# Value projection of 14 of 16 blocks by seven products in place of eight, woven with the gate matmuls

## The chip, the cores and the metric

One core of one Trainium2 chip. The metric is the device time of a whole launch in microseconds. Executions of one kernel mostly lie within 0.3% of each other on one chip, and the times compared below are of the same rounds on the same chip; where runs of different rounds are set beside each other, it is by their ratios to the kernel before. The span of a profile runs from the first to the last instruction and is some 2 us shorter than the time of the launch.

## The reference, cut to what matters

```python
# attention with projected keys and values: batch 8, 8 heads, 1024 positions, head 64
k_proj = np.einsum('ks,bhsd->bhkd', E, k);  v_proj = np.einsum('ks,bhsd->bhkd', F, v)
scores = 1/np.sqrt(64) * np.matmul(q, k_proj.transpose(0, 1, 3, 2))
attn = softmax(scores);  x = np.matmul(attn, v_proj)          # then 8192 tokens x 512
# gated feed-forward
gate = 1.0 / (1.0 + np.exp(-(x @ w_gate)))                     # 512 x 1536
val = x @ w_val                                                # 512 x 1536
out = gate * val @ w_out                                       # 1536 x 512
```

## The kernel before

The 8192 tokens are 16 blocks of 512, two blocks to a batch. Every operation is put on one list with the data that it reads and writes; each engine then runs its own part of that list in order and waits on semaphores where the data demand it. While TensorE works on the feed-forward of batch b, the attention of batch b + 1 is laid between its steps. PSUM, the memory that TensorE writes its products to, is used as eight banks: four for the feed-forward (`ffn`, shown as pF), four for the attention (`att`, shown as pA).

The step for one tile of 128 features makes gate and value with eight matmuls of 512 columns:

```python
def mstep(blk, m):
    pbs = {n: ffn.next() for n in "GV"}
    for n in "GV":
        for i in range(NI):                       # NI = 4
            mm_one(blk, m, i, n, pbs[n])          # W[:, i, m] x xT[:, i, half, 512 tokens]
    gate(blk, m, pbs["G"], pbs["V"])              # ScalarE: sig = tanh(0.5 g); VectorE: hT = (sig + 1) * v
```

The output projection of 14 blocks already goes by seven products: `first_products` and `last_products` make sums and differences of quarters of hT and w_out, run seven products of 12 matmuls of 256 columns in two banks, a and c, and copy a bank out between products of the same chain (`keep_snap` on ScalarE, `add_snap` on VectorE, into `ost`, which then is stored).

Keys and values of a batch are projected, copied and turned so:

```python
def kv(b, bk): ...                      # TensorE: 16 matmuls read the K and V buffers
def keep_kd(bk):
    act(kpd, bank[bk][0:64], ...)       # ScalarE: a copy of the projected keys
    add("SP", dma_start_transpose(kpD, kpd), dma="kpD")    # a small transposing transfer
# loads of the next K, V, Q: issued by GpSimd as soon as the buffers have been read
def load_k(b):
    load(KV[0], k[b]..., r=turned() if b >= 2 else ())     # also after the transposes of Q have landed
# [cut]
put(3, kv2)                             # batch 1: K/V product of batch 2, ahead of the output products
put(4 if b == 1 else 1, lambda: load_next(b + 2))
```

The softmax here doesn't subtract the row's maximum and nothing guards it: scores larger than these inputs give would overflow.

## Time and profile before

| | before |
|---|---|
| time, median of 3 (range) | 547.77 us (547.4 to 548.25) |
| span, granted clock | 545.4 us, 1.00 |
| TensorE, VectorE, ScalarE, GpSimd busy | 97%, 56%, 43%, 21% |
| one period (one batch) in the steady part | 64.6 us |

The page's busy line, the chain and TensorE's timeline stand in the prediction below. In a timeline a row is start, length, engine, line, operation, output <- inputs, shapes and count; in square brackets is how long the engine sat idle ahead of it and what released it. A hint for reading: matmul lengths overlap, so the pace is the difference of the starts.

### The profile page before, as it was taken

To read this page: it belongs to the slowest core of one execution; us is meant where nothing else is said; L and a number is where in the kernel's file an instruction comes from. 1 tells how busy PE (TensorE), PEld (TensorE's weight loads), DVE (VectorE), ACT (ScalarE), POOL (GpSimd) and SP (SyncE) were. 2 spreads that over 40 slices of the span, in tenths; PEclk is the share of its full clock that TensorE was granted. 3 is DMA by queue.
4 is the path that set the end of the run, shared out by engine and by line. 5 is a ranking of instruction groups with operands and counts; after the bars stand their busy time and mean duration, and the time that the engine had idled before them with its cause. 6 is when DMAs were issued, how large, how long until landed. Compare 5 with 4: busy or idle time off the path is not lost.

```text
span 545.4 us, 8923 instructions
## 1 busy us (share of the span) xinstructions
PE 530.7 (97%) x3504; PEld 298.7 (55%) x3561; DVE 305.5 (56%) x499; ACT 232.1 (43%) x414; POOL 113.5 (21%) x148
## 2 busy tenths in 40 slices
PE   5999999999999999999999999999999999999998
PEld 4544445646565474644647465564656547474654
DVE  4645386346863559437583466734785375834432
ACT  2654823465335633365333753346533562323330
POOL 9310200103800055000830019000350007100000
PEclk9999999999999999999999999999999999999999
DMA  9999998983795117960286502953020202001022
GB/s 159 200 195 201 163 209 176 153 178 49 148 201 127 31 21 150 152 156 11 79 137 131 121 12 78 185 144 59 13 78 1 78 0 81 2 7 72 1 77 78
DMA packets 76570, 56.09 MB, mean 103 GB/s; under 512 B 34704, under 2 KB 68240, under 8 KB 76528
## 3 DMA queue, kind: packets, MB, share of 16 engines
q0 software_dynamic: 33984, 29.89, 35.4%
q1 hardware_dynamic: 42544, 25.63, 18.6%
q8 instruction: 28, 0.46, 0.4%
q14 instruction: 14, 0.11, 0.1%
HBM read 60.29 MB, written 16.78 MB: 141 GB/s over the span
## 4 chain that ended last, share of the span: by engine, by line
PE 93%; DMA 2%; DVE 1%; ACT 1%; issue 1%; POOL 1%; POOLq 0%
PE pF L227 88%; PE pA L227 5%; DMA KV<-in_v_dram 2%; DVE hT L1063 0%; DVE rden L822 0%; POOL KV L245 0%; POOL Qb L245 0%; ACT xu L231 0%; ACT vpD L231 0%; ACT sig L231 0%; ACT eT L231 0%; ACT kpd L231 0%; DVE rden L602 0%; DVE hS L1138 0%; DVE xT L651 0%
## 5 line engine op out<-in xcount | busy, mean ns | idle before, releaser
L1063 DVE SCALAR_TENSOR_TENSOR hT<-sig,pF 128x512 bf16<-128x512 f32 x192 | 130.6, 681 | 118.9 <-PE pF L227 75.1
L227 PE MATMUL pF<-xT,wV 128*128 128x512 bf16 x752 | 195.6, 379 | 1.2 <-DVE hT L1063 0.3
L227 PE MATMUL pF<-xT,wG 128*128 128x512 bf16 x729 | 191.2, 379 | 3.1 <-issue 1.3
L231 ACT ACTIVATE sig<-pF 128x512 f32<-128x512 f32 x192 | 116.1, 605 | 171.2 <-PE pF L227 146.6
L896 POOL PARTITION_BROADCAST rb<-eT x96 | 77.1, 864 | 279.6 <-DMA eT<-rden 274.5
L227 PEld LDWEIGHTS pF<-xT,wV 128*128 128x128 bf16 x768 | 75.0, 98 | 90.9 <-DVE hT L1063 1.0
L227 PEld LDWEIGHTS pF<-xT,wG 128*128 128x128 bf16 x768 | 72.6, 98 | 88.6 <-issue 9.0
L227 PE MATMUL pF<-wO,hT 128*128 128x256 bf16 (+3 forms) x610 | 80.8, 287 | 0.1
L227 PEld LDWEIGHTS pF<-wO,hT 128*128 128x128 bf16 x612 | 59.2, 98 | 19.7 <-issue 0.8
L1183 DVE SCALAR_TENSOR_TENSOR ost<-pF,EF 128x512 f32<-128x512 f32 x28 | 19.4, 692 | 51.4 <-PE pF L227 48.8
L227 PE MATMUL pF<-wT,hT 128*128 128x256 bf16 x336 | 41.2, 273 | 0.0
L927 DVE TENSOR_TENSOR xT<-xu,rb 128x512 bf16<-128x512 f32 x48 | 40.3, 878 | 0.0
L227 PE MATMUL pF<-wT,hS 128*128 128x256 bf16 x336 | 39.0, 273 | 0.3 <-ACT EF L231 0.3
L231 ACT ACTIVATE EF<-pF 128x512 f32<-128x512 f32 x28 | 16.7, 597 | 47.0 <-PE pF L227 46.9
L227 PEld LDWEIGHTS pF<-wT,hT 128*128 128x128 bf16 x336 | 32.9, 98 | 6.8
L227 PEld LDWEIGHTS pF<-wT,hS 128*128 128x128 bf16 x336 | 32.8, 98 | 4.3 <-ACT EF L231 0.6
L822 DVE RECIPROCAL rden<-pA 128x128 f32<-128x128 f32 x26 | 24.6, 950 | 9.5 <-PE pA L227 9.5
L1183 DVE SCALAR_TENSOR_TENSOR ost<-pF,snap 128x512 f32<-128x512 f32 x14 | 9.7, 692 | 35.6 <-PE pF L227 25.0
L231 ACT ACTIVATE xu<-pA 128x512 f32<-128x512 f32 x46 | 25.2, 617 | 1.1 <-PE pA L227 1.1
L231 ACT ACTIVATE snap<-pF 128x512 f32<-128x512 f32 x14 | 8.4, 597 | 28.3 <-PE pF L227 28.3
L231 ACT ACTIVATE eT<-pA 128x512 bf16<-128x512 f32 x35 | 19.3, 622 | 1.0 <-PE pA L227 1.0
L231 ACT ACTIVATE eT<-pF 128x512 bf16<-128x512 f32 x29 | 15.8, 594 | 8.3 <-PE pF L227 8.2
(93 smaller groups left out, 268.5 us busy)
## 6 DMA issues: line engine op xcount, KB each, us to landing
out_dram<-ost SPq DMA_DIRECT2D x63, 256.0 KB, 2.4
Qb<-in_q_dram POOLq DMA_DIRECT2D x7, 1024.0 KB, 17.8
KV<-in_k_dram POOLq DMA_DIRECT2D x7, 1024.0 KB, 9.8
KV<-in_v_dram POOLq DMA_DIRECT2D x7, 1024.0 KB, 14.0
wO<-in_moe_w_out_dram POOLq DMA_DIRECT2D x1, 1536.0 KB, 11.9
wG<-in_moe_w_gate_dram POOLq DMA_DIRECT2D x5, 256.0 KB, 18.2
wV<-in_moe_w_val_dram POOLq DMA_DIRECT2D x5, 256.0 KB, 18.8
KV<-in_k_dram POOLq DMA_DIRECT2D x2, 512.0 KB, 8.8
```

The costliest lines, as they stand in the source:

```text
L227: return add("PE", lambda e: e.matmul(o, lhsT, rhs, **kw), r=r, x=[("bank", b)])
L231: return add("ACT", lambda e: e.activation(o, i, func, scale=scale), r=r, w=w, x=x)
L822: lambda e: e.reciprocal(rden[:, cc], bank[bk][:, cc]),
L896: lambda e, n=n, i=2 * rnd + c, j=j, parts=parts: e.partition_broadcast(rb[0:parts, n, :], rrow[32 * j : 32 * j + 1, i, :], channels=parts),
L927: lambda e: e.tensor_tensor(xT[s][:, r, :, 256 * g : 256 * g + 256], xu[:, n, :].rearrange("p (f c) -> p f c", f=2), y.rearrange("p (f c) ...
L1063: lambda e: e.scalar_tensor_tensor(hT[blk % 2][:, m, :], sg[:, :], 1.0, bank[pv][:, :], ALU.add, ALU.mult,),
L1183: lambda e: e.scalar_tensor_tensor(o, bank[bk][:, :].rearrange("p (j c) -> p j c", j=2), 0.5, snap[n].rearrange("p (j c) -> p j c", j=2), ...
```

## The change

The intent: values of a unit (four feature tiles of a block) by seven products of 4 matmuls of 256 columns in place of 16 matmuls of 512, from batch 1 on: 14 blocks x 3 units. With A the quarters of x and B the quarters of w_val, S1 = A21 + A22, S2 = S1 - A11, S3 = A11 - A21, S4 = A12 - S2, T1 = B12 - B11, T2 = B22 - T1, T3 = B22 - B12, T4 = B21 - T2. The products go into two banks a and c, between gate steps:

```diff
+        def v_pieces(K):          # condensed: several statements to a line
+            def p1():
+                v_product(blk, q, a, "A11", "B11", start=True);  v_snap(0, a)
+            def p26():
+                v_product(blk, q, c, "A12", "B21", start=True, stop=True);  v_add(0, c)
+                v_product(blk, q, a, "S2", "T2");  v_snap(1, a)
+                hidden(K, 0, 0, vsnap[0][:, :], [("vsnap", 0)])
+            def p57():
+                v_product(blk, q, c, "S1", "T1", start=True)
+                v_product(blk, q, a, "S3", "T3");  v_snap(2, a);  v_add(2, c)
+            def p4():
+                v_product(blk, q, a, "A22", "T4", stop=True)
+                hidden(K, 0, 1, bank[a][:, :], [], b=a);  hidden(K, 1, 1, vsnap[2][:, :], ...)
+            def p3():
+                v_product(blk, q, c, "S4", "B22", stop=True);  v_add(1, c)
+                hidden(K, 1, 0, vsnap[1][:, :], [("vsnap", 1)])
+                todo += [last_piece, p1, g_step(K, 1), p26, g_step(K, 2), p57,
+                         g_step(K, 3), p4, g_step(K + 1, 0)]; last_piece = p3
```

`v_snap` is a ScalarE copy of the bank, `v_add` a VectorE addition of bank and copy, `hidden` the gate multiply, now mostly with two SBUF operands. Sums of x (`xs_sums`), of w_val (`vt_sums`, once) and of hT (`s_sums`) all run on VectorE, most of them laid where TensorE runs the output products. To make room, the broadcast rows `rb` share the K/V buffer, early constants share one buffer, and the denominators go in eight groups. The schedule is written anew, and with it the start of batch 1 (condensed too):

```diff
-                put(3, kv2)
-                put(4 if b == 1 else 1, lambda b=b: load_next(b + 2))
+                on(0, 0, lambda: first_products(o0, first))
+                on(0, 2, lambda: last_products(o0))
+                    on(0, 2, kv2)
+                    on(0, 3, lambda: keep_kd(held_v["kv"]))
+                load_at = (1, 4) if b == 1 else (0, 2)
+                on(*load_at, lambda: (load_k(b + 2), load_v(b + 2), load_q(b + 2)))
+                on(4, 4, lambda: (mul(0, 0), mul(0, 1)))      # attention multiplies, unit 4
+                last = {-1: mul(1, 0), 0: (mul(1, 1), mul(2, 0), mul(2, 1)), 1: (mul(3, 0), mul(3, 1))}
```

(The first number of `on` is the unit within the batch, the second the slot within the unit. Of the full diff the buffers, the first batch and the helper functions are cut.)

## The prediction

> **What bounds the kernel now.** I read the page's busy line and chain first, then TensorE's timeline in one steady period, then what the other engines do there.
>
> ```profile
> PE 530.7 (97%) x3504; PEld 298.7 (55%) x3561; DVE 305.5 (56%) x499; ACT 232.1 (43%) x414; POOL 113.5 (21%) x148
> ...
> PE 93%; DMA 2%; DVE 1%; ACT 1%; issue 1%; POOL 1%; POOLq 0%
> ```
>
> The first line alone would not settle it, since a busy TensorE may still be badly fed. The second does: 93% of the chain that ended last is matmuls following matmuls, and 2% a load at the start. The chain repeats every 64.6 us (a mstep stretch starts at 187.92 and again at 252.51), one period for each batch, which is two blocks of values, gates and output plus the attention of the next batch. The timeline of TensorE (start, length, instruction) shows the pace inside:
>
> ```profile
> 257.48 2.78 PE L227 MATMUL pF<-wO,hT 128*128 128x256 bf16 x24
> 260.10 2.78 PE L227 MATMUL pF<-wT,hS 128*128 128x256 bf16 x24
> ...
> 274.42 1.03 PE L227 MATMUL pF<-xT,wV 128*128 128x512 bf16 x4
> 275.28 1.03 PE L227 MATMUL pF<-xT,wG 128*128 128x512 bf16 x4
> ```
>
> Read the starts, not the lengths. 24 matmuls of 256 columns take 260.10 - 257.48 = 2.62 us, 109.2 ns each. Four of 512 columns take 0.865 us (two such groups take 1.73), 216.2 ns each. There is no gap between groups. A period adds up: 192 x 0.2162 (gates and values) + 168 x 0.1092 (output products) = 41.5 + 18.3 = 59.9 us, and the remaining 4.7 us are the attention's own matmuls. So stalls are nearly nil and only fewer columns, without new gaps, can make it faster.
>
> **What the Trainium skill says.** "TensorE: Matmul & The Clock Gate", section Back-to-back issue gap, gives 518 cycles for 512 columns and 262 for 256 at 2.4 GHz, 216 and 109 ns: the trace agrees exactly, also with weights changed at every matmul. (Its sustained 131 ns at 512 columns is not seen here.) So two halves cost 1% more than a whole, and seven products keep nearly their 7/8. "SBUF — State Buffer", section Who interferes with whom, says that a VectorE instruction with two SBUF inputs contends with a GpSimd instruction that reads SBUF. The trace agrees, as the timelines of VectorE and GpSimd in the next period show:
>
> ```profile
> 333.77 1.97 DVE L927 TENSOR_TENSOR xT<-xu,rb 128x512 bf16<-128x512 f32 x2
> ...
> 340.75 1.29 DVE L927 TENSOR_TENSOR xT<-xu,rb 128x512 bf16<-128x512 f32 x2
> ```
>
> ```profile
> 332.81 6.21 POOL L896 PARTITION_BROADCAST rb<-eT  x7 [0.16 <-POOL rb L896]
> 339.09 0.90 POOL L245 DMA_DIRECT2D KV<-in_k_dram  x1
> ```
>
> Two multiplies take 1.97 us while GpSimd broadcasts and 1.29 after it: some 0.35 us more each. "VectorE: DVE Perf Modes", section The perf-mode tier table, puts tensor_tensor at double rate for bf16 in SBUF and single rate for fp32 or PSUM. The trace agrees: a sum of 768 bf16 elements takes 0.55 us, one pass over 512 fp32 elements 0.69.
>
> **The change part by part.** From batch 1 on a unit of work is four feature tiles of a block; there are 42 units (14 blocks x 3).
>
> *Removed and added on TensorE.* Values of a unit were 16 matmuls of 512 columns, 16 x 0.2162 = 3.46 us. They become 7 products x 4 matmuls of 256, 28 x 0.1092 = 3.06 us. Saved: 0.40 us a unit, 2.4 us of each 64.6 us period, **16.9 us** over 42 units. Gates, output products and attention keep their columns (the denominators go from 8 matmuls of 512 to 16 of 256, the same). If nothing waits: 547.8 - 16.9 = 530.9 us, 3.1% less. That is the ceiling.
>
> *Added on ScalarE.* Three copies of a bank a unit, 126 x 0.60 = 76 us: 232 to about 308 us, 58%. Not a bound.
>
> *Added on VectorE.* Three additions bank + copy a unit, each like the 0.69 us group: 126 x 0.69 = 87 us. The four gate multiplies of a unit stay four of the same size, but three of them now read two SBUF operands where before each read a bank. Operand sums for x, 56 of 512 bf16 elements at an estimated 0.4 (from 0.55 for 768): 22 us. Removed: half of the 24 reciprocals of batches 2 to 7, 12 x 0.95 = 11 us, and 12 small constants. Sum: 305 + 87 + 22 - 13 = about 400 us, plus the contention below: 76 to 78% of the span. Not a bound by its share, but it can be late.
>
> *Moved: the hand-overs.* This is what decides. In the old steps a bank came back only after the next step's work; now one accumulator is read by ScalarE or VectorE between two products of the same chain, three times a unit, and TensorE has only one gate step (0.865 us) or a gate step and a product (0.865 + 0.437 = 1.30) to fill the time. What a hand-over costs I take from the same stretch of the timeline:
>
> ```profile
> 257.48 2.78 PE L227 MATMUL pF<-wO,hT 128*128 128x256 bf16 x24
> 258.99 0.60 ACT L231 ACTIVATE EF<-pF 128x512 f32<-128x512 f32 x1 [1.38 <-PE pF L227]
> 260.10 2.78 PE L227 MATMUL pF<-wT,hS 128*128 128x256 bf16 x24
> 260.40 0.69 DVE L1183 SCALAR_TENSOR_TENSOR ost<-pF,EF 128x512 f32<-128x512 f32 x1 [1.51 <-PE pF L227]
> ```
>
> The first product is 12 matmuls, issued by 257.48 + 1.31 = 258.79; ScalarE starts 0.20 us later and takes 0.60. The second is issued by 260.10; VectorE starts 0.30 later and takes 0.69. With about 0.05 for the semaphore back (seen in the opening stretch), ScalarE's round trip is 0.85 us and VectorE's 1.04. Against the fill: first copy 0.85 of 1.30, second copy 0.85 of 1.30, first addition 1.04 of 1.30, second addition hidden under two gate steps: all fit. The **third copy** has 0.85 of 0.865, and the next weights should load 0.1 us earlier: I estimate 0.06 us lost a unit (0 to 0.15), 42 x 0.06 = **2.5 us**.
>
> *Sums in the unit.* Laying VectorE's program order against TensorE's, it is free for about 1.3 us after the first gate multiply of a unit (it waits for the third copy) and 0.3 us before the first addition. The change puts two short sums, or two of 1024 elements, in the first gap: they fit. The long ones lie at the output projection, where TensorE has 6.55 + 2.62 us of its own: they fit.
>
> *The multiplies of the attention.* From the reciprocals on, gather (8 small transfers instead of 4) and 16 broadcasts (13 us) fall on units 4 and 5 of a period. There each gate multiply with two SBUF operands takes some 0.35 us more, and two attention multiplies (1.97 us) sit in unit 4's gap of 1.3. I work out the second addition about 0.4 us late in unit 4, and in unit 5 the first snapshot addition of the output product, behind one more multiply, about 0.5 late: 0.9 us a period for 6 periods, **5.4 us**.
>
> *Loads.* The broadcast rows now share the K/V buffer, so the next loads are issued only once the multiplies are done. They have nearly three units and an output projection, some 29 us, before K and V are read; they landed in 9.8 and 14.0 us. Hidden. I add **1 us** for the transitions (vT and x sums in the first two batches).
>
> Sum: -16.9 + 2.5 + 5.4 + 1 = -8 us, 539.8. The schedule looks tuned by hand against such stalls (late copies split in halves, sums placed one by one), so I lean slightly lower: **539 us**.
>
> **The rivals.** (1) *All waits are hidden*: 531 to 534, faster by 2.5 to 3%. For it: margins are mostly 0.2 us or more and the old output products ran the same hand-over without a gap. Against it: the third copy's margin is 0.015 us, and the broadcasts. (2) *VectorE becomes the bound in units 4 and 5, or its late work passes on from unit to unit*: 543 to 552, no gain. For it: in those units it has about 7.3 us of work against 6.6 of TensorE's. Against: the output projection straight after gives TensorE 9 us in which VectorE catches up. (3) *A load or the gather comes late* because of the shared buffer: some us a period, 545 to 560. Against: 29 us for a landing of 14. (4) *Short groups with a wait each break the prefetch of weights*: 20 to 50 ns at 294 product groups, 6 to 15 us. Against: the gate groups of four also carry a wait and show no gap.
>
> **Range and chances.** Middle 539; low end 532 if nearly everything hides; high end 547 if (2) or (4) holds in part. Two per cent is 536.8 us, not far under my middle: faster 0.34, same 0.61, slower 0.05.
>
> **What the profile after would show.** Value matmuls 109 ns apart, and 1176 of them for 42 units; periods of 62.2 us plus stalls. The TensorE waits ahead of the fourth product (A22, T4) on ScalarE tell the third copy; waits on VectorE ahead of the last product of a unit and the S1, T1 output product, only in two units of six, tell the broadcasts. Multiplies of gates over 0.9 us while GpSimd is busy confirm the contention. VectorE near 400 to 420 us busy, ScalarE near 308. I am wrong if waits stand in every unit at VectorE's first addition, if periods of batch 7 (no attention) stall as much as the others, or if K/V or the transposes appear in the chain.

## More of the kernel before

The scores of batch 2 need kpD.

One stretch matters later, the start of batch 1, where keys of batch 2 are copied, turned and the loads of batch 3 are let go:

```profile
93.28 1.02 ACT L231 ACTIVATE kpd<-pA 64x1024 bf16<-64x1024 f32 x1 [2.08 <-PE pA L227]
...
94.63 2.31 SPq L743 DMA_TRANSPOSE kpD<-kpd  x1
...
96.72 0.88 POOL L245 DMA_DIRECT2D KV<-in_k_dram  x1 [32.23 <-PE pF L227]
...
106.31 0.41 PE L227 MATMUL pF<-qT,kpD 64*64 64x512 bf16 x4
```

The small transpose leaves at 94.63, two microseconds ahead of the first of three large loads at 96.72, and the scores come at 106.31 without a wait. Nothing in the kernel demanded that order: the load waited for the K/V product to have read its buffer and for the transposes of Q (`turned()`), the last of which landed at 95.86, but not for kpD. The small transpose landed after 3.9 us; the other five of its kind took 2.7.

## The result, and the profile after

| | before | after |
|---|---|---|
| time, median of 4 (range) | 547.61 us (547.4 to 548.25) | 549.56 us (549.04 to 550.39) |
| span of the profiled run, clock | 545.4 us, 1.00 | 547.7 us, 0.991 |

The ratio of after to before is 1.0035, 95% interval 1.0018 to 1.0052: no gain, a loss of a third of a per cent. From the page of the changed kernel:

```profile
PE 520.9 (95%) x4050; PEld 345.6 (63%) x4113; DVE 404.8 (74%) x655; ACT 300.3 (55%) x540; POOL 132.6 (24%) x148
...
PEclk9999999879999999999999999999999999999999
...
PE 86%; DVE 5%; DMA 5%; issue 2%; POOL 1%; SPq 1%; ACT 0%; DVEq 0%; POOLq 0%
```

VectorE and ScalarE are busy about as long as foreseen. Two things are new: transfers make up 5% of the chain, and the granted clock, level before, has a dent in the eighth and ninth slices, around 106 to 117 us. The pace of TensorE in the steady part is the expected one:

```profile
261.00 0.60 PE L264 MATMUL pF<-xS,wV 128*128 128x256 bf16 x4
261.44 0.60 PE L264 MATMUL pF<-xS,vT 128*128 128x256 bf16 x4
261.88 1.03 PE L264 MATMUL pF<-xT,wG 128*128 128x512 bf16 x4
262.74 0.60 PE L264 MATMUL pF<-xT,vT 128*128 128x256 bf16 x4
```

A product of four takes 261.44 - 261.00 = 0.44 us, and a gate step follows and is followed without a gap. So the matmuls cost what they should. A steady period, from one first gate step of a batch to the next, is 63.4 us (222.9 to 286.3) against 64.6 before: shorter by 1.2 us. The columns alone give 2.4; the prediction, less its 0.9 for the multiplies and 0.36 for the third copy, had 1.1. Counted from the weight load ahead of the first gate step of each batch, batches 2 to 5 take 63.39 us each where they took 64.59, batch 6 takes 62.47 where it took 62.74, and batch 7 with the end 72.25 where it took 73.19. The list of who waited, for TensorE:

```profile
PE pF L264 <- DMA kpD<-kpd: 6.4, 1, 6.4
PE pF L264 <- DVE vsnap L1435: 5.7, 9, 0.9
PE pA L264 <- DMA EF<-in_F_dram: 5.7, 1, 5.7
PE pA L264 <- DVE ost L1280: 1.5, 1, 1.5
```

Columns are total, times and longest. The third, at the very start, was there before (5.8 us). The other three are new: one wait of 6.4 us for a transfer, nine short ones for VectorE's additions, one of 1.5 us for an output buffer.

Setting equal points of work beside each other tells where the time is. These are the first gate steps of batches 1 and 2, before and then after:

```profile
84.29 1.03 PE L227 MATMUL pF<-xT,wG 128*128 128x512 bf16 x4
...
151.28 1.03 PE L227 MATMUL pF<-xT,wG 128*128 128x512 bf16 x4
```

```profile
83.59 1.03 PE L264 MATMUL pF<-xT,wG 128*128 128x512 bf16 x4
...
159.55 1.03 PE L264 MATMUL pF<-xT,wG 128*128 128x512 bf16 x4
```

**Batch 1 alone takes 75.96 us where it took 66.99**, 9 us longer, though it should have become 2.4 shorter: 11.4 us lost there. The timeline of all engines in that batch:

```profile
99.36 0.88 POOL L282 DMA_DIRECT2D KVs<-in_k_dram  x1 [36.19 <-PE pF L264]
...
100.21 1.00 ACT L268 ACTIVATE kpd<-pA 64x1024 bf16<-64x1024 f32 x1
...
101.24 1.65 SPq L780 DMA_TRANSPOSE kpD<-kpd  x1
...
110.51 0.64 PE L264 MATMUL pF<-qT,kpD 64*64 64x512 bf16 x4 [6.37 <-DMA kpD<-kpd]
...
112.77 1.91 PE L264 MATMUL pF<-xT,wG 128*128 128x512 bf16 x4
```

Compare with the four rows of before. The order has turned: the Q transposes left 3.3 us earlier and no longer hold the loads, which go out at 99.36, at the end of the K/V product, and the small transpose follows at 101.24, after the copy. It lands 9.2 us later (the median of all these transposes is 2.9), and TensorE, which reached the scores at 104.1, stands for 6.4 us. Then look at the last row: a gate step of four takes 1.91 us where it takes 1.03 elsewhere. TensorE's clock, in short stretches (columns: stretch, length, busy time and count for PE, PEld, DVE, ACT, POOL, clock, DMA share, GB/s):

```profile
106.00:106.50 0.50, 0.00 (x0) 0.00 (x0) 0.00 (x0) 0.00 (x0) 0.00 (x0) 0.89 1.19 196
106.50:107.00 0.50, 0.00 (x0) 0.00 (x0) 0.00 (x0) 0.00 (x0) 0.00 (x0) 0.50 1.24 200
...
116.00:116.50 0.50, 0.39 (x2) 0.27 (x2) 0.40 (x2) 0.01 (x1) 0.00 (x0) 0.50 1.26 211
116.50:117.00 0.50, 0.39 (x2) 0.21 (x2) 0.50 (x1) 0.50 (x2) 0.00 (x0) 0.87 1.24 207
```

The shares place the drop at 106.39 us, some 2.2 us into the idleness, and the rise at 116.63: 10.24 us at half clock, of which TensorE worked from 110.51 on. Six microseconds of work at half clock lose three. The Trainium skill has this in "TensorE: Matmul & The Clock Gate", section Part 1: The HAM clock gate: idleness over a window of about 3.4 us halves the clock and a busy window restores it. The stretch here is as long as three of its windows. So 6.4 + 3.0 + 1.5 for the store = 10.9 of the 11.4 us. The rest is about the size of the wait in unit 4, shown below. The prediction had 1 us for all transitions.

The 1.5 us are seen ahead of it, in the timeline of the same batch:

```profile
85.33 5.39 SPq L742 DMA_TRANSPOSE qT<-Qb  x4
...
90.77 0.57 SPq L1191 DMA_DIRECT2D out_dram<-ost  x1
...
94.56 0.69 DVE L1280 SCALAR_TENSOR_TENSOR ost<-pA,snap 128x512 f32<-128x512 f32 x1 [5.66 <-DMA out_dram<-ost]
...
95.31 1.48 PE L264 MATMUL pA<-wO,hT 128*128 128x256 bf16 x12 [1.53 <-DVE ost L1280]
```

A store of block 0 stood behind four transposes in the SyncE queue; the output product's addition had to wait until those rows of `ost` were free, and the last product for the addition.

In the steady part one wait returns in each period, at the end of unit 4, where GpSimd broadcasts: 0.73 us in five periods, 0.92 in the sixth.

```profile
268.74 2.10 DVE L949 TENSOR_TENSOR xT<-xu,KVs 128x512 bf16<-128x512 f32 x2 [0.69 <-POOL KVs L917]
...
270.76 0.68 DVE L1435 TENSOR_TENSOR vsnap<-pF,vsnap 128x512 f32<-128x512 f32 x1
...
271.50 0.61 PE L264 MATMUL pF<-xS,wV 128*128 128x256 bf16 x4 [0.74 <-DVE vsnap L1435]
```

The two attention multiplies wait 0.69 us for their row, take 2.10, and the addition behind them comes late for the last product.

### The profile page after: what moved, and what is told of

The parts are those of the page before. It is cut to its first block, busy times and chain, and to the rows that moved or that the text cites. A ratio compares the mean times of both kernels' runs of the same rounds, so it can differ in the third digit from the quotient of the medians.

```text
span 547.7 us, 10254 instructions
## 1 busy us (share of the span) xinstructions
PE 520.9 (95%) x4050; PEld 345.6 (63%) x4113; DVE 404.8 (74%) x655; ACT 300.3 (55%) x540; POOL 132.6 (24%) x148
## 4 chain that ended last, share of the span: by engine, by line
PE 86%; DVE 5%; DMA 5%; issue 2%; POOL 1%; SPq 1%; ACT 0%; DVEq 0%; POOLq 0%
PE pF L264 57%; PE pA L264 29%; DVE xT L949 2%; DMA kpD<-kpd 2%; DMA qT<-Qb 2%; DVE vsnap L1435 1%; DMA EF<-in_F_dram 1%; DMA out_dram<-ost 1%; POOL KVs L917 1%; DVE rden L841 1%; SPq L742 0%; DVE hT L1150 0%; DMA eT<-rden 0%; DVE hT L1416 0%; ACT vsnap L268 0%
## 5 line engine op out<-in xcount | busy, mean ns | idle before, releaser
L917 POOL PARTITION_BROADCAST KVs<-eT x96 | 95.9, 1025 | 257.9 <-PE pF L264 204.4
L1435 DVE TENSOR_TENSOR vsnap<-pF,vsnap 128x512 f32<-128x512 f32 x126 | 86.7, 688 | 47.7 <-PE pF L264 37.2
L268 ACT ACTIVATE vsnap<-pF 128x512 f32<-128x512 f32 x126 | 75.3, 597 | 54.0 <-PE pF L264 51.3
L1416 DVE SCALAR_TENSOR_TENSOR hT<-sig,vsnap 128x512 bf16<-128x512 f32 x126 | 88.5, 703 | 6.2 <-ACT vsnap L268 0.5
L264 PE MATMUL pF<-xT,wV 128*128 128x256 bf16 (+1 forms) x429 | 76.5, 299 | 0.5 <-DVE hT L1150 0.3
L264 PE MATMUL pA<-wO,hT 128*128 128x256 bf16 x504 | 59.6, 273 | 1.5 <-DVE ost L1280 1.5
L264 PE MATMUL pF<-xS,wV 128*128 128x256 bf16 x336 | 50.5, 273 | 5.8 <-DVE vsnap L1435 5.7
L264 PEld LDWEIGHTS pA<-wO,hT 128*128 128x128 bf16 x504 | 49.2, 98 | 7.7 <-DVE ost L1280 1.8
L264 PE MATMUL pF<-xS,vT 128*128 128x256 bf16 x336 | 50.9, 274 | 0.0
L1150 DVE SCALAR_TENSOR_TENSOR hT<-sig,pF 128x512 bf16<-128x512 f32 x24 | 16.4, 687 | 23.5 <-PE pF L264 12.2
```

Source lines behind the costliest of these rows:

```text
L264: return add("PE", lambda e: e.matmul(o, lhsT, rhs, **kw), r=r, x=[("bank", b)])
L268: return add("ACT", lambda e: e.activation(o, i, func, scale=scale), r=r, w=w, x=x)
L917: lambda e, n=n, i=2 * rnd + c, j=j, parts=parts: e.partition_broadcast(rb[0:parts, n, :], rrow[32 * j : 32 * j + 1, i, :], channels=parts),
L1150: lambda e: e.scalar_tensor_tensor(hT[blk % 2][:, m, :], sg, 1.0, bank[pv][:, :], ALU.add, ALU.mult,),
L1416: lambda e: e.scalar_tensor_tensor(o, sg[:, :, cc], 1.0, x.rearrange("p (j c) -> p j c", j=2), ALU.add, ALU.mult,),
L1435: lambda e: e.tensor_tensor(o, bank[bk][:, :], o, ALU.add),
```

## The experiments

The theory: the products gain what they should, and the hand-over to batch 1 takes it back: the loads of batch 3, let go by the K/V product itself, hold up the small transpose; the standstill then halves the clock; a store behind transposes adds 1 to 3 us; and in the steady part the two multiplies of unit 4 cost another half of the gain. Rivals: the transpose is late for another reason (its own queue, or its place in the program); the slow stretch has nothing to do with the standstill; VectorE is simply full.

**K load after kpD.**

```diff
-                r=turned() if b >= 2 else (),
+                r=(turned() if b >= 2 else []) + ([("kpD", 0)] if b == 3 else []),
```

> One edit to the changed kernel: the K load of batch 3 also waits until kpD of batch 2 has landed. Theory (the three loads issued at 99.4 to 102 us hold up the small kpD transpose, 9.2 us to landing against 2.7; TensorE idles 6.4 us and then runs at clock 0.50 for some 5 us): the transpose lands within 3.5 us, the 6.4 us wait and the slow clock go, 538 to 541 us, clock 1.00; perhaps 1 us comes back where K and V of batch 3 are now read later. Rival (the transpose is slow because stores and transposes stand before it in its own queue, or because it is late at all): the landing stays near 9 us and the time near 549.

Measured: 542.91 us (540.74 to 544.89) against 546.71 of before in the same rounds, ratio 0.9937 (0.9905 to 0.9968).

```profile
101.82 1.19 SPq L780 DMA_TRANSPOSE kpD<-kpd  x1
...
104.66 0.41 PE L264 MATMUL pF<-qT,kpD 64*64 64x512 bf16 x4
...
105.38 0.88 POOL L282 DMA_DIRECT2D KVs<-in_k_dram  x1 [42.01 <-PE pA L264]
```

The transpose leaves 0.6 us later than in the changed kernel and yet lands after 2.67 us, and the scores start at 104.66, without a wait; no transpose of this kind took over 3.8 us. The stores ahead of it in its own queue are there as in the changed kernel, so that rival falls. The later loads were in time: the K/V product of batch 3 stands at 120.54 without a gap. The median lies above the expected 538 to 541; the profiled run had 540.74 and clock 1.00, the other three 0.997. What halved the clock for a moment in those three is not traced. The store's wait, which was still there, is the likely cause: in the trace of the run with the multiplies spread (below) such a wait of 2.46 us was followed by 3.41 us at half clock, from 97.78 to 101.19, which is just 0.003 of the mean clock, and with the store moved as well the clock was 1.00 in every run.

**The same loads one unit later in the program.**

```diff
-                load_at = (1, 4) if b == 1 else (0, 2)
+                load_at = (2, 4) if b == 1 else (0, 2)
```

> The changed kernel with the three loads for batch 3 put one unit later in the program order (unit 2 instead of unit 1), no new dependency. Theory (GpSimd runs its own list and the loads go out as soon as the K/V product of batch 2 has read its buffer, wherever they stand): issue still at 99.4 us, kpD still 9 us, 549.5 us. Rival (the place in the program sets the time): loads some 7 us later, kpD lands in 3 us, about 540 us.

Measured: 549.56 us (547.66 to 552.28), ratio 1.005 (1.0014 to 1.0086).

```profile
100.59 0.88 POOL L282 DMA_DIRECT2D KVs<-in_k_dram  x1 [36.10 <-PE pF L264]
...
111.82 0.64 PE L264 MATMUL pF<-qT,kpD 64*64 64x512 bf16 x4 [6.44 <-DMA kpD<-kpd]
```

The loads still go out when the K/V product has read its buffer, and the wait stands. In this kernel, where an operation is written matters only against others of its own engine, and on GpSimd nothing stood in between. A dependency or an earlier transpose can set this order, as the first run above and the last below show.

**Warm matmuls in the standstill.** 110 matmuls on the identity ahead of the scores of batch 2, into a free bank:

```diff
+                    def warm():
+                        bk = AA.take()
+                        for _ in range(110):
+                            mm(bk, bank[bk][:, 0:P], ident[:, :], ident[:, :], ["ident"])
+                        AA.append(bk)
+                    on(1, 0, warm)
```

> The changed kernel with 110 idle-filling 128-column matmuls (about 6.1 us at full clock) on the identity ahead of the scores of batch 2, where TensorE now idles 6.4 us for kpD; the wait itself stays. Theory (idleness halves the granted clock, which costs some 3.3 us after the wait): clock 1.00, kpD lands as late as before, 545.5 to 547 us. Rival (the slow stretch has another cause, such as the busy DMA or the mix of work): clock stays 0.99 and the time 549 to 550.

Measured: 547.86 us (546.63 to 550.61), ratio 1.0022 (0.9988 to 1.0056), clock 1.00 in three of four runs and 0.997 in one.

```profile
106.06 6.30 PE L264 MATMUL pA<-ident 128*128 128x128 bf16 x110
112.44 0.41 PE L264 MATMUL pF<-qT,kpD 64*64 64x512 bf16 x4
...
113.66 1.03 PE L264 MATMUL pF<-xT,wG 128*128 128x512 bf16 x4
```

The transpose was as late as before (9.1 us to landing), but the gate step after it takes 1.03 us and the clock never falls there. So the standstill is what halves the clock. The time misses the expected 545.5 to 547: it is 1.7 us under that of the kernel with the loads moved (which behaves as the changed kernel), not 3 under, and the ranges overlap: in this trace the store's wait was 2.9 us in place of 1.5. The effect on the clock is shown, its worth in time only roughly.

**Store ahead of the transposes.**

```diff
-        put(24, transpose_q)
+        put(25, transpose_q)
```

> One edit to the changed kernel: the four qT transposes of batch 2 are put behind the store of the last oproj tile of block 0 instead of ahead of it. Theory (the store waited 5.4 us in its queue behind the transposes, and the output product's addition waits for that store to leave the same rows of ost): the 1.5 us TensorE wait at 95.3 us goes; 547.5 to 548.5 us; the kpD wait stays. Rival (the wait is VectorE's own lateness from the sums laid there): nothing changes, 549.5.

Measured: 546.66 us (546.03 to 548.11), ratio 0.9997 (0.9975 to 1.0019). TensorE's wait on `ost` is gone, the 5.9 us for kpD stay. The gain, 2.9 us under the run with the loads moved, is more than the 1 to 2 expected; the wait varies from run to run: 1.1, 1.5, 2.1, 2.5 and 2.9 us in the traces of the five kernels that still had it.

**Both repairs.**

> The changed kernel with both repairs of the hand-over to batch 1 (K load after kpD, store ahead of the transposes). Theory (the two waits and the slow clock are all that separates the change from its steady gain): TensorE's waits on kpD and on the store both gone, clock 1.00 in every run, 3 us under the first repair alone and 6 to 8 us under the kernel before: ratio 0.985 to 0.990. Rival (the waits of the two overlap, or K and V of batch 3 come late now): no better than the first repair alone, 0.993.

Measured: 538.56 us (537.68 to 538.69) against 547.61, ratio 0.9832 (0.9817 to 0.9848), clock 1.00 in every run. With these two edits of a line each the change is worth 1.7%, 9 us, somewhat more than the 6 to 8 expected. VectorE does the same work here (404.8 us busy), so a full VectorE was not what held the changed kernel back. The first repair alone had 0.9937, so the two do not overlap. The profiled run left no clock record; its longest matmuls for the scores, 376 and 400 ns where the half clock of the changed kernel gave 631 and 632, show full clock too.

**Multiplies spread.** In the changed kernel, one multiply of unit 4 is moved into the output product and the others each one place on:

```diff
-                on(4, 4, lambda: (mul(0, 0), mul(0, 1)))
-                    -1: mul(1, 0), 0: (mul(1, 1), mul(2, 0), mul(2, 1)), 1: (mul(3, 0), mul(3, 1))
+                on(4, 4, lambda: mul(0, 0))
+                    -1: mul(0, 1), 0: (mul(1, 0), mul(1, 1), mul(2, 0)), 1: (mul(2, 1), mul(3, 0), mul(3, 1))
```

> The changed kernel with one of the two attention multiplies of unit 4 moved into the stretch of the output product, the later ones each one place on; nothing else. Theory (two multiplies under the broadcasts make VectorE's addition to the second bank 0.9 us late once a period): the wait ahead of the last product of unit 4 falls from 0.9 to 0.1 us, 4 to 5 us less over 6 periods, ratio about 0.996 against before. Rival (VectorE is full over units 4 and 5, and the lateness only moves to the output product): within 1 us of the changed kernel, 1.003 to 1.005.

Measured: 548.57 us (545.65 to 549.45), ratio 1.0006 (0.9982 to 1.003). The expected 4 to 5 us are not to be seen. By its time alone this run decides nothing, since the unrepaired hand-over spreads it over 4 us; in its trace the store's wait had grown to 2.5 us, with a slow stretch of its own. But TensorE's waits on these additions fell from 5.7 us in nine to 1.1 in three. The next run shows what that is worth where the noise is gone.

**All three.**

> The changed kernel with the K load after kpD, the store ahead of the transposes and the multiplies spread. Theory: the three gains add up, about 10 + 2.5 + 4.5 us under the changed kernel, 532 to 535 us where before is 547, ratio 0.974 to 0.980. Rival (spread multiplies give nothing): as the two repairs alone, 0.985 to 0.990.

Measured: 535.24 us (535.0 to 536.99), just above the expected range, ratio 0.9782 (0.9764 to 0.98), clock 1.00 in every run. The list of waits:

```profile
PE pA L264 <- DMA EF<-in_F_dram: 5.8, 1, 5.8
PE pF L264 <- DVE vsnap L1435: 1.1, 3, 0.6
```

Against both repairs alone (0.9832) the spread multiplies give 0.5%, 2.7 to 3.3 us, less than the 4.5 expected. A period is now 62.9 us (the same VectorE addition of unit 4 starts at 257.49 and at 320.38), 0.7 from the 62.2 that the columns allow.

**K/V product of batch 2 ahead of the output product**, with the store and the multiplies as above, in place of the new dependency:

```diff
-                    on(0, 2, kv2)
-                    on(0, 3, lambda: keep_kd(held_v["kv"]))
+                on(0, 0, kv2)        # with keep_kd at its end, ahead of first_products(o0, first)
```

> Store ahead of the transposes, the multiplies spread, and instead of the new dependency the K/V product of batch 2 and its copy put ahead of the output product of block 1, so that kpD leaves before the loads do. Theory: kpD lands in about 3 us or well before the scores, the loads still go out before 96 us, clock 1.00, ratio 0.975 to 0.982. Rival: the early K/V product only moves the same collision (the qT transposes and kpD leave together with the loads), and 3 to 6 us are lost again.

Measured: 535.52 us (535.43 to 536.2), ratio 0.9785 (0.977 to 0.98). The transpose left at 91.11, ahead of the first load at 95.17, and landed after 3.8 us; no other of its kind took over 4.3. A second way to part the transpose from the loads gives the same time, which speaks for the collision itself and not for some side effect of the dependency. Nor is it peculiar to transposes: four stores issued beside these loads, at 96.28 to 98.49, took 7.4 to 9.4 us to land (median of all stores 2.4), but nothing waited for them. Both versions beat the kernel before by 2.2% and, by the ratios, the changed one by 2.5%.

## Why the prediction was wrong

By its own steps:

- *Removed and added on TensorE: 16.9 us.* Right. The products run at 0.44 us each, and with the three repairs batch 1 is 2.5 us shorter than before and the profiled span 11.9. By the same count of batches what is missing to 16.9 is 0.7 us in each of batches 2 to 5, 1.6 in batch 6 and 1.5 in batch 7 (0.4 of it the last product of batch 6, which this count puts there), less 0.8 by which the part ahead of batch 1 was shorter.
- *The transitions: 1 us.* **This is the step that failed.** It was put down for the sums of the first two batches, and those cost nothing to be seen (batch 0 is as long as before, and batch 1 with the repairs has its full gain). The hand-over to batch 1 cost 10.9 us: 6.4 for the transpose, 3.0 for the halved clock, 1.5 for the store. I looked at when the loads would be *needed* and found them hidden; I did not ask what their earlier release would run into. The profile of before had the answer in two rows, the transpose at 94.63 and the load at 96.72: a margin of 2 us that nothing enforced, in a stretch that the change rewrote.
- *Loads hidden.* True of the loads themselves; none was waited for. The third rival (a load or the gather late because of the shared buffer) named the wrong transfer and the wrong cause: the buffer's sharing played no part in batch 1. Its range, 545 to 560 us, and that of the second, 543 to 552, hold the measured time by luck.
- *The third copy: 2.5 us.* Too much. The weight load waited, TensorE did not: PEld waited for the copies 42 times, 13.8 us in all, but in the trace of both repairs the step ahead of the fourth product is longer than its four matmuls by no more than 0.35 us in all 42 units.
- *The multiplies: 0.9 us a period.* About right in size, not quite in place: one wait of 0.73 to 0.92 us before the last product of unit 4, none at the output product that followed. Beside broadcasts a gate multiply with two SBUF operands took 0.91 us at most, not the estimated 1.04; in return a broadcast grew from 864 to 1025 ns on average. That the steady period comes out so near the forecast (1.2 us gained, 1.1 foreseen) is luck in part: the third copy cost next to nothing, and smaller waits took its place.
- *Batch 7.* Short waits for VectorE in its units as well, 0.28, 0.21 and 0.11 us of idleness; by the starts of the matmuls they cost 1.1 us in the run with all repairs. In the first two, sums of hT lie ahead of the late addition. Not foreseen; that batch 7 loses nearly as much as a steady period (1.2) was one of the prediction's signs of being wrong. Another came true outright: transposes stand in the chain, kpD with 2% and qT with 2%.
- *VectorE 400 to 420 us, ScalarE near 308.* Measured 404.8 and 300.3.
- *The clock.* Not considered: the prediction counted any standstill at its own length.

With the failed step at its measured 10.9 us in place of 1 the same sum gives about 549.7. This is a check of where the miss lay and no proof, since the small cost of the third copy would lower it again by 2.2 and the start of batch 1 by 0.7, and the waits of batch 7 would raise it by 1.

The theory of the hand-over is shown: each of its three parts vanished with its own edit, and the two repairs together brought 2.0% or 11 us (ratios 1.0035 and 0.9832). What is argued and not shown is how the loads hold up the transpose inside the DMA engines.

## What to carry to other kernels

When a change rewrites a schedule, look in the old profile for small transfers that leave just ahead of large ones and ask what enforces that order; if it is luck, add the dependency. In a kernel built like this one, a place in the program orders an operation only against those of its own engine. And count a standstill of several microseconds in a matmul kernel at more than its length, since the work after it may run at half clock: here 6.4 us of standing cost 3.0 more.

## What the Trainium skill lacked or had wrong

- "TensorE: Matmul & The Clock Gate", section Part 1: The HAM clock gate: the trace agrees on the length (10.24 us at half clock, three windows of 3.413 us; 6.83 and 3.41 us in other runs). But the clock fell already 2.2 us after the last matmul, and in another run after a wait of only 2.46 us, under the "≥1 idle window (~3.4µs)" of its table; a wait of 2.86 us (warm matmuls) left it at full. How much work in a window still counts as idle no page says.
- Same page, section Back-to-back issue gap: a "sustained roofline" of 131 ns at 512 columns is nowhere to be seen in weight-changing streams; they run at 216 ns (and 109 at 256), the formula that the page calls isolated.
- "DMA: Bandwidth & Descriptors", section Queues, rings and completion order: engines take turns between queues packet by packet. No page says what that does to the landing of a small transfer beside loads from another queue: the transpose took 9.2 us beside three loads of 1 MB each and 2.67 ahead of them.
- "SBUF — State Buffer", section SBUF: two separate sides: the loser of the shared port is said to block until the other's whole instruction is done. Here a multiply that started at 268.74, beside a broadcast from 268.57 to 269.37, took 1.03 us; alone it takes 0.68, and blocked to the end of the broadcast it would have taken 1.31. Spans on GpSimd are rough in the profile, so this is a hint and no proof. Broadcasts grew from 864 to 1025 ns on average when 126 more two-operand VectorE instructions came in.
